# Placing the cluster rows of q and k by ScalarE in a routed-attention and expert-layer kernel

## The chip, the core and the metric

The kernel runs on one core of a Trainium2 chip. Its time is the device time in microseconds (us) of one execution, as a median of several. The core has five engines that this text names: TensorE (PE in the profile, with its weight loads apart as PEld), VectorE (DVE), ScalarE (ACT), GpSimd (POOL) and SyncE (SP), which here issues transfers. A letter q after an engine (ACTq, SPq) is its queue of instructions that don't compute, such as the issue of a transfer.

## The reference: what is computed

Two layers, one behind the other. The first is attention of 4 batches, 8 heads, 768 positions and 64 dimensions, in which a query sees only the keys of its own cluster. The cluster of a row of q or k is the nearest of 16 centroids of its head:

```python
q_assign = np.argmax(np.einsum('bhsd,hcd->bhsc', q_n, c_n), axis=-1)
k_assign = np.argmax(np.einsum('bhsd,hcd->bhsc', k_n, c_n), axis=-1)
mask = q_assign[:, :, :, None] == k_assign[:, :, None, :]
scores = scale * np.matmul(q, k.transpose(0, 1, 3, 2))
scores = np.where(mask, scores, -1000000000.0)
scores = scores - np.max(scores, axis=-1, keepdims=True)
attn = np.exp(scores)
attn = attn / (np.sum(attn, axis=-1, keepdims=True) + 1e-09)
return np.matmul(attn, v).astype(np.float32)
```

The second sends each of the 3072 rows that come out (512 wide) to one of 8 experts, two matrices with a relu between them, and scales the row by its gate. The change touches the first layer only.

## The kernel before

The attention works on 16 **groups**: a group is one batch and a pair of heads `a`. A group has 12 **units**, a unit being 128 keys against half of the queries (384) of both heads, and the units are worked in **turns** of six, so a group has two turns: turn 2g and turn 2g + 1. A turn is six scores, then the jobs of part 0, then six products with v, then the jobs of part 1:

```python
for n in range(-4, NTURN + 5):
    for x in range(n * NB, (n + 1) * NB):
        if 0 <= x < NU:
            score(x)
    for f, a in jobs.get((n, 0), ()):
        f(*a)
    for x in range(n * NB, (n + 1) * NB):
        if 0 <= x < NU:
            attend(x)
    for f, a in jobs.get((n, 1), ()):
        f(*a)
```

Each engine works through its own instructions in the order of this program.

The mask is a matmul. For each head, tile `ohT` holds in 32 partitions the one-hot cluster of every query, and for every key a large negative number everywhere but in its own cluster, where it is zero. A score is the product of q and k plus the product of these, then an exp:

```python
def score(u):
    ...
    ps = ps_s.tile([P, 2, 512], F32, name="sps")        # three buffers
    for a in range(2):
        r = slice(a * D, (a + 1) * D)
        nc.tensor.matmul(ps[:, a, 0:HS], lhsT=qk[g][r, 1, ks], rhs=qk[g][r, 0, qs], start=True, stop=False)   # L959
    for a in range(2):
        r = slice(a * D, (a + 1) * D)
        nc.tensor.matmul(ps[:, a, 0:HS], lhsT=ohT[g][r, 1, ks], rhs=ohT[g][r, 0, qs], start=False, stop=True) # L962
    A[u] = ap.tile([P, 2, HS], F32, name="A")
    nc.scalar.activation(A[u], ps[:, :, 0:HS], AF.Exp, scale=D**-0.5)                                         # L964
    ...  # T, the sum of A over the units of a half, by VectorE (L967, L971)
```

`attend` is the product with v (L979), `finish` ScalarE's copy of the product O out of its accumulator (L987).

The clusters come from `similar` (products with the centroids, brought out by VectorE as `sim`), `assign` and `assign2` (the largest of 16, as one-hot). They end in a tile `ohs` of 128 partitions: 32 for each of q and k and each half of the positions, with both heads side by side. To come into `ohT` the rows have to be put at other partitions, and for k the numbers have to be made of the one-hot: `big` holds a scale and a bias for each partition and head, which leave the other head's rows zero.

```python
def places(half, a):
    return slice(half * 32, half * 32 + 32), slice(a * D, a * D + 32), slice(half * HS, (half + 1) * HS)

def put_q(g):
    ohT[g] = ohTs[g % 2]
    for half in range(2):
        for a in range(2):
            i, r, cols = places(half, a)
            nc.sync.dma_start(out=ohT[g][r, 0, cols], in_=sims[g][i])                      # L917

def put_k(g):
    t, kv = sims.pop(g), asg.tile([P, 2, HS], BF16, name="kv")
    for a in range(2):
        nc.vector.tensor_scalar(                                                           # L923
            kv[D:P, a, :], t[D:P], scalar1=big[D:P, a, 0:1], scalar2=big[D:P, a, 1:2], op0=ALU.mult, op1=ALU.add
        )
    for half in range(2):
        for a in range(2):
            i, r, cols = places(half + 2, a)
            nc.sync.dma_start(out=ohT[g][r, 1, (half * HS) : (half + 1) * HS], in_=kv[i, a, :])  # L929
```

Group 0 has no transfers: `put` has ScalarE copy its four pieces of q (L939) and VectorE make its four of k.

The schedule of the jobs, as far as it matters here:

```python
for g in range(NG):
    n = g * TG                                   # TG = 2 turns a group
    ...
    elif g == 1:
        at(-2, 1, idle_of, 20)
        at(0, 0, turn_blocks, g)
        for f in (similar, assign, assign2, put_q, put_k):
            at(0, 1, f, g)
    else:
        at(n - 3, 0, turn_blocks, g)
        at(n - 2, 0, similar, g)
        at(n - 2, 0, assign, g)
        at(n - 2, 1, assign2, g)
        at(n - 2, 1, put_q, g)
        at(n - 2, 1, put_k, g)
    at(n, 1, finish, g, 0)
    at(n + 1, 1, finish, g, 1)
    if g < NG - 1:
        at(n + 2, 0, weigh, g)
        at(n + 2, 1, keep, g, 0, S)
        if g % HP == HP - 1:                     # the last pair of heads of a batch
            at(n + 3, 0, gate, g // HP)
            at(n + 3, 1, keep_pads, g // HP)
...
for e in range(2):
    for i in range(DB):                          # turns 5, 7, ... 19
        at(HP * TG * (e + 1) - 4 + 2 * i + 1, 0, early, e, i)
```

`early` has ScalarE issue two loads of expert weights (L1177). `gate` has VectorE take the largest logit and subtract (L1039, L1041), ScalarE exponentiate (L1044), and VectorE go on.

Of the kernel before, what the change touches and what calls it, by code (L numbers as in the profile page):

```python
# [9 lines left out]
BF16 = mybir.dt.bfloat16  # L10
I32 = mybir.dt.int32
AX = mybir.AxisListType.X
AF = mybir.ActivationFunctionType
ALU = mybir.AluOpType
# [171 lines left out]
def kernel(  # L186
# [11 lines left out]
    nc = tc.nc  # L198
    B, H, S, D = q.shape
    C = centroids.shape[1]  # L200
    P = 128
# [5 lines left out]
    HS = S // 2  # L207
# [25 lines left out]
    def fetch1(e, i):  # L233
        w1 = wpool.tile([P, DB, F], F32, name=f"w1_{i % 2}")
        nc.sync.dma_start(out=w1, in_=moe_w1[bass.ds(e, 1)].rearrange("e (a p) f -> p (e a) f", p=P))
        return w1

    def fetch2(e, i):
        w2 = wpool.tile([P, FB, Dm], F32, name=f"w2_{i % 2}")
        nc.sync.dma_start(out=w2, in_=moe_w2[bass.ds(e, 1)].rearrange("e (a p) d -> p (e a) d", p=P))  # L240
        return w2
# [459 lines left out]
    with ExitStack() as actx:  # L701
# [3 lines left out]
        asg = actx.enter_context(tc.tile_pool(name="asg", bufs=2))  # L705
# [78 lines left out]
        for i in range(2):  # L784
            t = ohp.tile([P, 2, S], BF16, name=f"ohT{i}")
            nc.gpsimd.memset(t, 0.0)
            ohTs.append(t)
        for a in range(2):
            r = slice(a * D, (a + 1) * D)
# [20 lines left out]
        for a in range(2):  # L810
# [6 lines left out]
            part_i, part_i, scalar1=4, scalar2=1, op0=ALU.arith_shift_right, op1=ALU.bitwise_and  # L817
        )
        big = consts.tile([P, 2, 2], F32)
# [14 lines left out]
        qk, sims, ohT = {}, {}, {}  # L834
# [72 lines left out]
        def places(half, a):  # L907

            return slice(half * 32, half * 32 + 32), slice(a * D, a * D + 32), slice(half * HS, (half + 1) * HS)

        def put_q(g):

            ohT[g] = ohTs[g % 2]
            for half in range(2):
                for a in range(2):
                    i, r, cols = places(half, a)
                    nc.sync.dma_start(out=ohT[g][r, 0, cols], in_=sims[g][i])  # L917

        def put_k(g):

            t, kv = sims.pop(g), asg.tile([P, 2, HS], BF16, name="kv")
            for a in range(2):
                nc.vector.tensor_scalar(  # L923
                    kv[D:P, a, :], t[D:P], scalar1=big[D:P, a, 0:1], scalar2=big[D:P, a, 1:2], op0=ALU.mult, op1=ALU.add
                )
            for half in range(2):
                for a in range(2):
                    i, r, cols = places(half + 2, a)
                    nc.sync.dma_start(out=ohT[g][r, 1, (half * HS) : (half + 1) * HS], in_=kv[i, a, :])  # L929

        def put(g):

# [127 lines left out]
        def at(n, part, f, *a):  # L1060
            jobs.setdefault((n, part), []).append((f, a))
# [8 lines left out]
        for g in range(NG):  # L1070
            n = g * TG
            if g == 0:
                at(-4, 0, turn, g, 0)
                at(-4, 0, load_next)
                at(-4, 0, blocks)
                at(-4, 1, turn, g, 1)
                at(-3, 0, similar, g)
                at(-3, 0, assign, g)
                at(-3, 0, assign2, g)
                at(-3, 0, put, g)  # L1080
            elif g == 1:
                at(-2, 1, idle_of, 20)
                at(0, 0, turn_blocks, g)
                for f in (similar, assign, assign2, put_q, put_k):
                    at(0, 1, f, g)
            else:
                at(n - 3, 0, turn_blocks, g)
                at(n - 2, 0, similar, g)
                at(n - 2, 0, assign, g)
                at(n - 2, 1, assign2, g)  # L1090
                at(n - 2, 1, put_q, g)
                at(n - 2, 1, put_k, g)
            at(n, 1, finish, g, 0)
            at(n + 1, 1, finish, g, 1)
            if g < NG - 1:
                at(n + 2, 0, weigh, g)
                at(n + 2, 1, keep, g, 0, S)
                if g % HP == HP - 1:
                    at(n + 3, 0, gate, g // HP)
                    at(n + 3, 1, keep_pads, g // HP)  # L1100
# [41 lines left out]
        n = (NG - HP) * TG  # L1142
# [13 lines left out]
        n = NG * TG  # L1156
# [46 lines left out]
    with tc.tile_pool(name="sm", bufs=1) as sm:  # L1203
# [20 lines left out]
        for part in parts:  # L1224
            n, over = part["n"], part["over"]
# [8 lines left out]
        for t0 in range(0, NT, TQ):  # L1234
# [34 lines left out]
            op0=ALU.is_ge, op1=ALU.add,  # L1269
# [53 lines left out]
    g = groups[0]  # L1323
# [49 lines left out]
    with tc.If(more > 0):  # L1373
        nx = nc.values_load(xe[0:1, NX : NX + 1], min_val=0, max_val=NX)
        general = nc.values_load(xe[0:1, NX + 1 : NX + 2], min_val=0, max_val=1)
        with tc.If(nx > XU):
            with ExitStack() as ectx:
# [3 lines left out]
                with tc.For_i(XU, nx, 1) as i:  # L1381
# [4 lines left out]
                    g = dict(  # L1386
                        n=[P], rows=N, w=(fetch1(ex, 0), fetch2(ex, 0)), gi=lambda j: gi[:, 0:1], si=lambda j: gi[:, 1:2], apart=False
                    )
# [37 lines left out]
```

## Time and profile before

| | |
|---|---|
| time, median of 3 | 713.92 us (713.08 to 714.17) |
| profiled span | 717.3 us, mean granted TensorE clock 0.994 |
| attention, 16 to 346 us | PE busy 323.30, DVE 279.01, ACT 166.78 of 330 us |
| ohT transfers | 60 from ohs, 60 from kv, 24 KB each, median 5.2 and 3.0 us to landing |
| kv on VectorE (L923) | 30 operations, median 386 ns |

A line of a group in the profile has: line of the program, engine, operation, what is written from what, shapes (partitions x elements), count | busy us, mean ns of one | idle us of the engine just before them, and what ended it. A line of waits has: who waited <- for whom, total us, times, longest us. A line of a timeline has: start us, us, engine, line, operation, count, and in brackets the idle time before it and its releaser.

### The profile page before, as it was taken

Reading aid. Unit: us, or ns where it says so; the run is one execution under the profiler, and the core shown is the slowest. Engines: PE = TensorE matmul, PEld = TensorE weight load, DVE = VectorE, ACT = ScalarE, POOL = GpSimd, SP = SyncE. Lnnn points to the kernel's source line nnn. Section 1 sums busy time; section 2 is a strip of 40 time slices with the busy share of each in tenths; the row PEclk is TensorE's granted clock in tenths of the full one; section 3 lists DMA queues with packets and bytes.
Section 4 is the critical chain, followed back from the end, with each engine's and each line's share of the span. In section 5 each row is a group of like instructions: output and inputs, shape, how many; then the busy total and the mean of one; then the engine's idle time right before and its main releaser. Section 6 shows DMA issues by size and latency. Waiting matters only on the chain.

```text
span 717.3 us, 12233 instructions
## 1 busy us (share of the span) xinstructions
PE 695.1 (97%) x4723; PEld 453.0 (63%) x4723; DVE 478.3 (67%) x761; ACT 255.8 (36%) x403; POOL 170.8 (24%) x262
## 2 busy tenths in 40 slices
PE   8999989999999999999999999999999999999993
PEld 6445444444444444545656969878798787888761
DVE  5898878798898889997456466565755667554200
ACT  3555445445544556445212222312214131231200
POOL 4022112222221122245235312112121221110101
PEclk9999999999999999999999999999999999999997
DMA  7355686668877555313135547485575855568440
GB/s 144 67 97 98 134 142 132 115 127 150 154 146 147 100 100 79 57 28 77 27 118 183 159 174 287 154 285 207 203 271 186 298 207 203 220 230 296 153 134 20
DMA packets 144164, 109.58 MB, mean 153 GB/s; under 512 B 106337, under 2 KB 114273, under 8 KB 144098
## 3 DMA queue, kind: packets, MB, share of 16 engines
q1 hardware_dynamic: 131042, 80.32, 41.5%
q0 software_dynamic: 7488, 19.57, 11.1%
q10 hardware_dynamic: 5568, 8.83, 4.3%
q8 instruction: 39, 0.64, 0.4%
q14 instruction: 27, 0.22, 0.1%
HBM read 93.01 MB, written 13.25 MB: 148 GB/s over the span
## 4 chain that ended last, share of the span: by engine, by line
PE 69%; issue 11%; DVE 8%; DMA 4%; SPq 3%; POOL 2%; ACT 1%; ACTq 0%; POOLq 0%; DVEq 0%
PE sps L959 12%; PE O L979 11%; PE sps L496 10%; PE sps L328 9%; PE sps L518 9%; PE sps L384 8%; PE sps L962 3%; DVE T L971 3%; DMA ohT<-kv 2%; PE sps L364 2%; PE mps L1002 2%; PE sps L309 2%; DMA k_in<-in_k_dram 1%; PE sps L873 1%; POOL out_dram L348 1%
## 5 line engine op out<-in xcount | busy, mean ns | idle before, releaser
L959 PE MATMUL sps<-qk 64*128 64x384 f32 x768 | 160.6, 494 | 1.4 <-DVE sim L880 1.4
L964 ACT ACTIVATE A<-sps 128x768 f32<-128x768 f32 x192 | 149.9, 814 | 20.9 <-PE sps L962 16.9
L971 DVE TENSOR_TENSOR T<-T,A 128x768 f32<-128x768 f32 x128 | 122.6, 958 | 14.6 <-DVE T L971 1.0
L979 PE MATMUL O<-A,v_in 128*64 128x384 f32 x768 | 130.9, 490 | 0.0
L959 PEld LDWEIGHTS sps<-qk 64*128 64x128 f32 x768 | 67.4, 186 | 52.4 <-issue 42.6
L979 PEld LDWEIGHTS O<-A,v_in 128*64 128x64 f32 x768 | 52.3, 137 | 74.0 <-issue 73.9
L962 PE MATMUL sps<-ohT 64*128 64x384 bf16 x384 | 67.0, 323 | 5.0 <-DMA ohT<-kv 5.0
L348 POOL DMA_INDIRECT out_dram<-zo,s_idx x32 | 33.4, 1043 | 154.1 <-ACT zo L344 93.6
L282 POOL DMA_INDIRECT xg<-x_rows,g_idx x32 | 38.1, 1189 | 115.6 <-ACT gate L302 65.1
L384 PE MATMUL sps<-w,h_sb 128*128 128x512 f32 x144 | 63.1, 592 | 0.0
L987 ACT COPY xT<-O 128x384 f32<-128x384 f32 x32 | 15.3, 478 | 132.8 <-PE O L979 100.3
L328 PEld LDWEIGHTS sps<-xgT,w 128*128 128x128 f32 x512 | 58.3, 192 | 4.5 <-issue 2.5
L328 PE MATMUL sps<-xgT,w 128*128 128x128 f32 x512 | 58.7, 275 | 0.0
L1014 POOL COPY dens<-ls 128x12 f32<-128x12 f32 x16 | 3.1, 194 | 211.9 <-DVE ls L1010 211.9
L1032 POOL DMA_DIRECT2D x_rows<-xb x68 | 48.4, 719 | 10.8 <-DVE xb L1029 8.8
L967 DVE SCALAR_TENSOR_TENSOR T<-A 128x768 f32<-128x768 f32 x32 | 30.6, 957 | 25.3 <-ACT A L964 24.8
L384 PEld LDWEIGHTS sps<-w,h_sb 128*128 128x128 f32 x144 | 26.7, 190 | 30.6 <-issue 30.6
L962 PEld LDWEIGHTS <-ohT 64*128 64x128 bf16 x384 | 22.1, 94 | 32.8 <-DMA ohT<-kv 10.4
L496 PEld LDWEIGHTS sps<-xs,w1s 128*128 128x128 f32 x288 | 36.0, 190 | 4.2 <-DVE xs L407 4.2
L496 PE MATMUL sps<-xs,w1s 128*128 128x144 f32 x288 | 37.8, 288 | 0.0
L344 ACT ACTIVATE zo<-sps,gate 128x512 f32<-128x512 f32 x12 | 8.2, 687 | 72.1 <-PE sps L384 53.5
L518 PE MATMUL sps<-w2s,hs 128*128 128x256 f32 x144 | 33.6, 383 | 0.0
(254 smaller groups left out, 905.4 us busy)
## 6 DMA issues: line engine op xcount, KB each, us to landing
w<-in_moe_w_dram SPq DMA_DIRECT2D x28, 2048.0 KB, 9.0
w<-in_moe_w_dram ACTq DMA_DIRECT2D x16, 512.0 KB, 5.6
v_in<-in_v_dram SPq DMA_DIRECT2D x16, 384.0 KB, 3.9
q_in<-in_q_dram SPq DMA_DIRECT2D x60, 96.0 KB, 3.5
k_in<-in_k_dram SPq DMA_DIRECT2D x60, 96.0 KB, 3.8
x_rows<-xb POOLq DMA_DIRECT2D x60, 96.0 KB, 4.4
ohT<-ohs SPq DMA_DIRECT2D x60, 24.0 KB, 5.2
ohT<-kv SPq DMA_DIRECT2D x60, 24.0 KB, 3.0
```

Source lines behind the costliest of these rows:

```text
L282: nc.gpsimd.indirect_dma_start(out=g["xg"][0:m, j, :], out_offset=None, in_=x_d[0 : g["rows"], :], in_offset=bass.IndirectOffsetOnAxis(ap= ...
L328: nc.tensor.matmul(o, lhsT=g["w"][0][:, c, fb * P : (fb + 1) * P], rhs=g["xT"][:, c, :cols], start=(c == 0), stop=(c == DB - 1),)
L348: ins = nc.gpsimd.indirect_dma_start(out=out[:, :], out_offset=bass.IndirectOffsetOnAxis(ap=g["si"](j)[0:m], axis=0), in_=zo[0:m], in_offs ...
L384: nc.tensor.matmul(zp, lhsT=g["h"][:, fb, j * P : (j + 1) * P], rhs=g["w"][1][:, fb, :], start=(fb == 0), stop=(fb == FB - 1),)
L496: nc.tensor.matmul(o, lhsT=a[:, c, f * P : (f + 1) * P], rhs=b[:, c, :], start=(c == 0), stop=(c == KH - 1),)
L518: nc.tensor.matmul(ps[:, 0, 0:DH], lhsT=a[:, f, :], rhs=b[:, f, :], start=(f == 0), stop=(f == FH - 1),)
L959: nc.tensor.matmul(ps[:, a, 0:HS], lhsT=qk[g][r, 1, ks], rhs=qk[g][r, 0, qs], start=True, stop=False)
L962: nc.tensor.matmul(ps[:, a, 0:HS], lhsT=ohT[g][r, 1, ks], rhs=ohT[g][r, 0, qs], start=False, stop=True)
L964: nc.scalar.activation(A[u], ps[:, :, 0:HS], AF.Exp, scale=D**-0.5)
L971: nc.vector.tensor_tensor(T[g, half], T[g, half], A[u], op=ALU.add)
L979: nc.tensor.matmul(O[g, half][a * D : (a + 1) * D, 0:HS], lhsT=rows[g, "v"][:, a, j, :], rhs=a_[:, a, :], start=(j == 0), stop=(j == NQ - 1),)
L1032: nc.gpsimd.dma_start(out=x_d[b * S + c0 : b * S + c1, d0 : d0 + 32].rearrange("(n t) d -> t n d", t=32), in_=xb[quad * 32 : (quad + 1) * ...
```

## The change

The cluster rows of q and k are no longer moved by transfers. ScalarE places them: a copy for each of the four pieces of q, and for each of the four pieces of k an activation (identity) that applies scale and bias of `big` on the way, so that VectorE makes no `kv`. It does so a turn later than the transfers were issued, in the second turn of the group ahead, behind that turn's six exponentials, where the engines' order has TensorE at the products with v and ScalarE waiting for them. It is meant to take the landing time of small transfers out of the way of the mask's matmul, and two operations a group off VectorE.

```diff
-        def put_q(g):
-
+        def put_by_scalar(g):
+
+            t = sims.pop(g)
             ohT[g] = ohTs[g % 2]
             for half in range(2):
                 for a in range(2):
                     i, r, cols = places(half, a)
-                    nc.sync.dma_start(out=ohT[g][r, 0, cols], in_=sims[g][i])
-
-        def put_k(g):
-
-            t, kv = sims.pop(g), asg.tile([P, 2, HS], BF16, name="kv")
-            for a in range(2):
-                nc.vector.tensor_scalar(
-                    kv[D:P, a, :], t[D:P], scalar1=big[D:P, a, 0:1], scalar2=big[D:P, a, 1:2], op0=ALU.mult, op1=ALU.add
-                )
-            for half in range(2):
-                for a in range(2):
-                    i, r, cols = places(half + 2, a)
-                    nc.sync.dma_start(out=ohT[g][r, 1, (half * HS) : (half + 1) * HS], in_=kv[i, a, :])
+                    k = slice(D + half * 32, D + half * 32 + 32)
+                    nc.scalar.copy(ohT[g][r, 0, cols], t[i])
+                    nc.scalar.activation(
+                        ohT[g][r, 1, cols], t[k], AF.Identity, scale=big[k, a, 0:1], bias=big[k, a, 1:2]
+                    )
...
             elif g == 1:
                 at(-2, 1, idle_of, 20)
                 at(0, 0, turn_blocks, g)
-                for f in (similar, assign, assign2, put_q, put_k):
+                for f in (similar, assign, assign2):
                     at(0, 1, f, g)
+                at(1, 0, put_by_scalar, g)
             else:
                 at(n - 3, 0, turn_blocks, g)
                 at(n - 2, 0, similar, g)
                 at(n - 2, 0, assign, g)
                 at(n - 2, 1, assign2, g)
-                at(n - 2, 1, put_q, g)
-                at(n - 2, 1, put_k, g)
+                at(n - 1, 0, put_by_scalar, g)
```

## The prediction

> **What bounds the kernel now.** I read the page first (busy shares, then groups), then the waits, then TensorE's and ScalarE's timelines of the attention part, which runs from about 16 to 346 us. On the page:
>
> ```profile
> PE 695.1 (97%) x4723; PEld 453.0 (63%) x4723; DVE 478.3 (67%) x761; ACT 255.8 (36%) x403; POOL 170.8 (24%) x262
> ...
> L962 PE MATMUL sps<-ohT 64*128 64x384 bf16 x384 | 67.0, 323 | 5.0 <-DMA ohT<-kv 5.0
> ```
>
> TensorE is the bound, and the only gaps in it that this change can reach are those ahead of L962, the matmul that adds the cluster mask. The waits of the span, and then TensorE's alone:
>
> ```profile
> ACT xT L987 <- PE O L979: 100.3, 24, 5.0
> ...
> PEld L962 <- DMA ohT<-kv: 10.4, 11, 2.5
> ```
> ```profile
> PE sps L962 <- DMA ohT<-kv: 5.0, 3, 1.9
> ...
> PE sps L959 <- DVE sim L880: 1.4, 1, 1.4
> ```
>
> ScalarE idles 100 us before its 24 copies of O, up to 5.0 us each: that is the room the change wants to use. TensorE's timeline shows the worst stall, at the start of group 4:
>
> ```profile
> 95.37 0.92 PE L959 MATMUL sps<-qk 64*128 64x384 f32 x4
> 98.19 0.54 PE L962 MATMUL sps<-ohT 64*128 64x384 bf16 x2 [1.91 <-DMA ohT<-kv]
> ```
>
> A group is two turns of six units. From TensorE's timeline, an undisturbed second turn takes 9.06 us (191.23 to 200.29: scores 5.04, products with v 4.02); the first adds weigh and similar, 10.82 us; a group is 19.88. Groups 1 to 15 start at 35.36, 55.47, 75.47, 95.37, 117.61, 138.00, 160.01, 180.10, 200.29, 220.18, 240.49, 260.38, 280.27, 300.70 and 323.01, and the last ends at 345.38. What each has over 19.88, less extra matmuls (0.54 in groups 13 and 14; +1.38 of turns and -0.65 of similar in the last) and less the 1.44 behind DVE's sim, is what the transfers cost: 0.23, 0.12, 0.02, 2.36, 0.51, 2.13, 0.21, 0.31, 0.01, 0.43, 0.01, 0.01, 0.01, 0.4, 1.75. **Sum 8.5 us**, 1.2% of the time: the ceiling of the direct gain.
>
> ScalarE around the start of group 9:
>
> ```profile
> 191.34 0.48 ACT L987 COPY xT<-O 128x384 f32<-128x384 f32 x1 [4.98 <-PE O L979]
> 192.37 4.82 ACT L964 ACTIVATE A<-sps 128x768 f32<-128x768 f32 x6 [0.55 <-PE sps L962]
> 200.24 0.24 ACT L1044 ACTIVATE ex<-ex 128x48 f32<-128x48 f32 x1 [3.04 <-DVE ex L1041]
> 200.32 0.84 ACTq L1177 DMA_DIRECT2D w<-in_moe_w_dram  x2
> 201.20 0.48 ACT L987 COPY xT<-O 128x384 f32<-128x384 f32 x1 [0.72 <-DMA ohT<-kv]
> 201.57 4.74 ACT L964 ACTIVATE A<-sps 128x768 f32<-128x768 f32 x6
> ```
>
> The exponentials of the second turn end 5.96 us after its start (197.19); the next are due 10.3 to 10.5 after it. The window is so some 4 us, with one copy (0.37 to the next start) in it. In this turn the gate's exp sits inside the window and waits for VectorE until 200.24, the window's end.
>
> **What the Trainium skill says.** "ScalarE: Activation LUTs", section "What ACT_TABLE_LOAD costs": each per-partition pointer for scale or bias adds about 93 ns to an ACTIVATE, and back-to-back ones overlap by about 93 ns. The groups of ScalarE by form agree on the first: 687 ns with a gate pointer, 594 without, the same shape. Section "Table sets: the hidden batching unit": identity and copy are in every set, so no table load; the trace has only its two loads at the start (1283 ns each), though it copies and exponentiates throughout. "DMA: Bandwidth & Descriptors", "Anatomy of one DMA — SWDGE (gpsimd) path": a semaphore wait happens on the issuing sequencer before dispatch. The trace agrees: the weight loads issued by ScalarE (L1177) start only once a kv transfer has landed (98.00 for the stall above), and hold the copy behind them.
>
> **The change, part by part.**
>
> *Removed:* 15 x 8 transfers, so the 8.5 us above; and two DVE operations per group, 15 x 0.80 = 12 us of VectorE. VectorE is not the bound: only its one late sim (1.44) is on the path, and kv work of 0.88 in the turn before plus the slack from below removes it. **Gain 8.5 + 1.4 = 9.9 us.**
>
> *Added:* eight ScalarE operations of 32x384 in one piece. From the groups by form, and from ScalarE's timeline for the same copies in group 0:
>
> ```profile
> L338 ACT ACTIVATE h_sb<-sps 128x512 f32<-128x512 f32 x16 | 8.7, 594 | 44.5 <-PE sps L328 44.5
> ...
> L344 ACT ACTIVATE zo<-sps,gate 128x512 f32<-128x512 f32 x12 | 8.2, 687 | 72.1 <-PE sps L384 53.5 <-issue 12.4 <-PEq L1373 6.2
> L344 ACT ACTIVATE zo<-zc,gate 32x512 f32<-32x512 f32 x8 | 5.8, 722 | 17.4 <-DVE zc L374 17.4
> ...
> L939 ACT COPY ohT<-ohs 32x384 bf16<-32x384 bf16 x4 | 2.0, 510 | 6.3 <-DVE ohs L905 6.2
> ...
> L338 ACT ACTIVATE hs<-sps 128x288 f32<-128x288 f32 x8 | 2.8, 408 | 12.0 <-PE sps L328 12.0
> ```
> ```profile
> 14.82 2.11 ACT L939 COPY ohT<-ohs 32x384 bf16<-32x384 bf16 x4 [6.23 <-DVE ohs L905]
> ```
>
> Four copies in 2.11 us: (2.11 - 0.51) / 3 = 0.533 from start to start, no overlap. The k operation: 722 (SBUF, one pointer, 512 long), less 128 x 0.83 (from 594 and 408 at 512 and 288), plus 93 for the second pointer = 709 ns, and the same 24 ns of gap: 0.733. Eight: 4 x 0.533 + 4 x 0.733 = **5.06 us**, more than the window.
>
> *What follows on the path.* In an ordinary group the eight end 5.96 + 5.06 = 11.02 after the second turn's start, the copy of O moves the first exp to 11.42, which is 2.36 into the next turn. TensorE has three score buffers: the fourth score starts 0.90 after the first exp starts (181.95 to 182.85 in group 8) and is due 2.52 into the turn (193.75 - 191.23), so an exp up to 1.62 in is free. Loss 2.36 - 1.62 = 0.74. The exps then follow closer (0.72) than scores (0.81), so it does not grow.
> - Groups 1, 2, 11, 12, 14: 5 x 0.74 = 3.7.
> - Groups 3, 4, 6, 7, 8, 10 also issue two weight loads after the eight. Transfers take eight completion counters in turn, so each waits for the one eight before it: today an ohT transfer, after the change a load long landed. So they no longer wait; they start 0.08 after the operation ahead of them starts, so of 0.84 only some 0.2 shows: 6 x 0.94 = 5.6.
> - Groups 5, 9, 13: the gate's exp is ahead of the eight in program order (it is appended for an earlier group, in the same part of the same turn). Its VectorE input ends at 117.87, 200.20, 279.84; without kv the chain of T additions starts earlier, but the first cannot start before the second exp's end (111.39, 194.07, 274.05), which saves 0.8, 0.57, 0.22. The exp so ends about 8.7 to 8.8 after the turn's start, the eight 13.8, the first exp at 14.2 to 14.5: losses 3.75, 3.65, 3.5 = 10.9. TensorE's first mask matmul, due at 9.8, waits there too, till about 11.2, inside the same loss.
> - Group 15: TensorE's own extras leave 0.2.
>
> **Sum: 3.7 + 5.6 + 10.9 + 0.2 = 20.4 lost, 9.9 gained: +10.5 us, 724.4.**
>
> **Rivals.**
> 1. *The operations overlap* by 0.1 each, as 128-row ones do (exps at 0.72 of 0.81). Then the eight take 4 x 0.41 + 4 x 0.61 = 4.08, ordinary groups lose nothing, the gates 0.98 less each, 8.0 in all; 9.9 gained: 712. Against it: all three pairs of exactly these copies show a gap of 24 ns.
> 2. *Only one pointer costs*, 0.64 a k operation: eight in 4.69, losses 5 x 0.37, 6 x 0.57 and 9.8: 15.1 lost, 719.
> 3. *As intended*: the gate's exp does not hold the eight (its input early, or another order): those three then lose 0.74 to 0.94 as others do, 12.1 in all, 716; with overlap as well, 704. Against: the 3.04 us wait at 200.24 is in the trace, and ScalarE runs in order.
> 4. *VectorE the bound*: its 12 us would count in full, 702. Against: it idles in each first turn waiting for A (22.6 us in all), so what it saves it waits.
>
> **Range and chances.** I give the sum above some two thirds, the cheaper rivals the rest: **722 us**, range 712 to 728. Over 2% slower needs 728.2, a dearer operation than any seen (each 0.1 us on the pitch adds 0.8 in 14 groups, 11 us): 0.09. Over 2% faster needs 699.6, more than all waits named: 0.02. Within: 0.89.
>
> **What would show it.** Right: no wait of L962 on a transfer; k operations near 0.7 us; the first exp of an ordinary group 2.3 to 2.4 us into its first turn, and TensorE held there by A; in groups 5, 9, 13 the eight start after the gate's exp, and L962 waits for ScalarE. Wrong: eight operations in 4 us; a gate's exp behind the eight; TensorE's groups at 19.9 throughout.

## The result, and the profile after

The changed kernel takes **727.01 us** (median of 4, 726.92 to 727.11) against 714.04 us (713.08 to 715.05) before: ratio 1.0181, 95% interval 1.0164 to 1.0199. It is slower by 13.0 us. The profiled spans, 717.3 us before and 725.4 after, differ by 8.1 only; the experiment "again" below settles why.

The page after: engines first, then the groups of the scores, of the mask's matmul, of ScalarE's copy of O and of the k operations. The columns are those of before; L952, L955, L957 and L980 are what L959, L962, L964 and L987 were.

```profile
PE 696.4 (96%) x4723; PEld 449.8 (62%) x4723; DVE 465.6 (64%) x731; ACT 324.6 (45%) x523; POOL 170.0 (23%) x262
...
L952 PE MATMUL sps<-qk 64*128 64x384 f32 x768 | 160.8, 496 | 10.3 <-ACT A L957 10.3
...
L955 PE MATMUL sps<-ohT 64*128 64x384 bf16 x384 | 64.7, 323 | 2.7 <-ACT ohT L920 2.7
...
L980 ACT COPY xT<-O 128x384 f32<-128x384 f32 x32 | 15.3, 478 | 80.6 <-PE O L972 80.2
...
L920 ACT ACTIVATE ohT<-ohs,big 32x384 bf16<-32x384 bf16 x60 | 42.0, 700 | 0.8
```

ScalarE is busy for 68.8 us more, VectorE for 12.7 less, TensorE as long as before. TensorE's waits show the exchange: none behind a transfer any more, and two behind ScalarE.

```profile
PE sps L952 <- ACT A L957: 10.3, 14, 1.7
PE sps L955 <- ACT ohT L920: 2.7, 3, 0.9
```

ScalarE's timeline over the start of group 12, which has neither a gate nor weight loads in its way. The second turn of group 11 starts on TensorE at 258.15, group 12 at 267.21.

```profile
259.26 4.85 ACT L957 ACTIVATE A<-sps 128x768 f32<-128x768 f32 x6 [0.52 <-PE sps L955]
264.14 0.51 ACT L919 COPY ohT<-ohs 32x384 bf16<-32x384 bf16 x1
264.67 0.70 ACT L920 ACTIVATE ohT<-ohs,big 32x384 bf16<-32x384 bf16 x1
265.39 0.51 ACT L919 COPY ohT<-ohs 32x384 bf16<-32x384 bf16 x1
...
268.39 0.70 ACT L920 ACTIVATE ohT<-ohs,big 32x384 bf16<-32x384 bf16 x1
269.12 0.48 ACT L980 COPY xT<-O 128x384 f32<-128x384 f32 x1
269.49 4.41 ACT L957 ACTIVATE A<-sps 128x768 f32<-128x768 f32 x6
```

The eight stand from 264.14 to 269.09, 4.95 us, while TensorE's products with v take 4.02. The first exp of the new group starts 2.28 us into it. TensorE's timeline shows what that does: the fourth score, the first that needs a buffer back, starts 0.87 us after that exp.

```profile
267.21 0.92 PE L952 MATMUL sps<-qk 64*128 64x384 f32 x4
...
270.36 0.92 PE L952 MATMUL sps<-qk 64*128 64x384 f32 x4 [0.46 <-ACT A L957]
```

It starts 3.15 us into the turn and not 2.52, and its first pair of matmuls, behind the pause, takes another 0.10 us (587 ns each for 482). Ordinary groups take 20.61 or 20.62 us (group 2 20.69) where an undisturbed one takes 19.89.

In groups 5, 9 and 13 the gate's exp is ahead. ScalarE's timeline at the start of group 9, then TensorE's (the second turn of group 8 starts at 193.79):

```profile
194.91 4.86 ACT L957 ACTIVATE A<-sps 128x768 f32<-128x768 f32 x6 [0.52 <-PE sps L955]
202.16 0.24 ACT L1037 ACTIVATE ex<-ex 128x48 f32<-128x48 f32 x1 [2.39 <-DVE ex L1034]
202.31 0.49 ACT L919 COPY ohT<-ohs 32x384 bf16<-32x384 bf16 x1
...
204.07 0.84 ACTq L1170 DMA_DIRECT2D w<-in_moe_w_dram  x2
...
206.54 0.70 ACT L920 ACTIVATE ohT<-ohs,big 32x384 bf16<-32x384 bf16 x1
207.27 0.48 ACT L980 COPY xT<-O 128x384 f32<-128x384 f32 x1
207.64 4.47 ACT L957 ACTIVATE A<-sps 128x768 f32<-128x768 f32 x6
```
```profile
202.86 0.92 PE L952 MATMUL sps<-qk 64*128 64x384 f32 x4
...
204.82 0.33 PE L955 MATMUL sps<-ohT 64*128 64x384 bf16 x1 [0.89 <-ACT ohT L920]
...
208.51 0.92 PE L952 MATMUL sps<-qk 64*128 64x384 f32 x4 [1.75 <-ACT A L957]
```

ScalarE idles 2.39 us in the very window the change wants to fill, and then does the eight when the next group has begun. The mask's matmul waits for the rows, and the fourth score for its buffer: the group takes 23.12 us.

### The profile page after: what moved, and what is told of

Read it like the earlier page. It is cut to its first block, busy times and chain, and to the rows that moved or that the text cites. A ratio compares the mean times of both kernels' runs of the same rounds, so it can differ in the third digit from the quotient of the medians.

```text
span 725.4 us, 12157 instructions
## 1 busy us (share of the span) xinstructions
PE 696.4 (96%) x4723; PEld 449.8 (62%) x4723; DVE 465.6 (64%) x731; ACT 324.6 (45%) x523; POOL 170.0 (23%) x262
## 4 chain that ended last, share of the span: by engine, by line
PE 73%; issue 10%; ACT 7%; DVE 5%; POOL 2%; DMA 1%; ACTq 0%; SPq 0%; POOLq 0%; DVEq 0%
PE sps L952 13%; PE O L972 13%; PE sps L496 10%; PE sps L328 9%; PE sps L518 9%; PE sps L384 8%; ACT A L957 3%; PE sps L955 3%; DVE T L964 3%; PE mps L995 2%; PE sps L364 2%; PE sps L309 2%; PE sps L873 1%; ACT ohT L920 1%; ACT ohT L919 1%
## 5 line engine op out<-in xcount | busy, mean ns | idle before, releaser
L952 PE MATMUL sps<-qk 64*128 64x384 f32 x768 | 160.8, 496 | 10.3 <-ACT A L957 10.3
L957 ACT ACTIVATE A<-sps 128x768 f32<-128x768 f32 x192 | 147.1, 818 | 12.4 <-PE sps L955 11.2
L964 DVE TENSOR_TENSOR T<-T,A 128x768 f32<-128x768 f32 x128 | 122.6, 958 | 14.3 <-ACT ohT L920 0.5
L952 PEld LDWEIGHTS sps<-qk 64*128 64x128 f32 x768 | 66.0, 186 | 67.6 <-issue 37.8
L955 PE MATMUL sps<-ohT 64*128 64x384 bf16 x384 | 64.7, 323 | 2.7 <-ACT ohT L920 2.7
L980 ACT COPY xT<-O 128x384 f32<-128x384 f32 x32 | 15.3, 478 | 80.6 <-PE O L972 80.2
L920 ACT ACTIVATE ohT<-ohs,big 32x384 bf16<-32x384 bf16 x60 | 42.0, 700 | 0.8
L955 PEld LDWEIGHTS <-ohT 64*128 64x128 bf16 x384 | 20.1, 94 | 28.6 <-ACT ohT L920 4.7
```

Of the source, the lines that this page charges most:

```text
L920: nc.scalar.activation(ohT[g][r, 1, cols], t[k], AF.Identity, scale=big[k, a, 0:1], bias=big[k, a, 1:2])
L964: nc.vector.tensor_tensor(T[g, half], T[g, half], A[u], op=ALU.add)
```

## The experiments

Theory A: TensorE waits for ScalarE's chain in the second turn (the eight, the copy of O, the exp), and where the gate's exp stands ahead of the eight the chain starts late. Rivals: B, the added ScalarE work costs as such, wherever it stands; C against D, on why medians and profiles differ; E, the loss is capped; F, VectorE is the bound. Ratios are to the kernel before in the same batch of runs; that kernel's own median was between 713.9 and 716.2 us. The changed kernel was timed in an earlier batch, so what a run gains on it is given by the profiled spans too.

**The kernel before, once more.** No edit.

> The kernel before, unchanged, profiled once more. The change gained +8.1 us by the two profiled spans (717.3 to 725.4) but +13.0 by the medians. Theory C: the profiled execution of before that the prediction was read from had some 5 us more of stalls behind the ohT transfers than most executions have, because landings vary from execution to execution. Then a new profile has a span of 711 to 714 us and its groups have 3 to 5 us in all over 19.88 us each, instead of 8.5. Rival D: a profiled execution of before is slower everywhere or always stalls as much. Then the span is 717 again with 8 to 9 us of stalls, or the extra lies outside the attention.

Measured: 715.64 us beside 716.16 (ratio 0.9996, 0.9988 to 1.0004), a span of 713.5 us. TensorE's waits:

```profile
PE sps L962 <- DMA ohT<-kv: 2.9, 3, 1.5
PE sps L959 <- DVE sim L880: 1.6, 1, 1.6
```

Worked out as in the prediction, from group starts, the transfers cost 4.8 us here, where the profile it read had 8.5: group 4 takes 21.48 us and not 22.24, group 6 20.49 and not 22.01, and five groups that had lost 0.2 to 0.5 lose nothing. The attention as a whole is 3.5 us shorter and the span 3.8. The transfers land sooner, at most 6.4 (from ohs) and 4.2 us (from kv) after their issue instead of 7.8 and 5.7. C holds: the stalls behind the transfers differ from execution to execution, and the profile of before was a bad one. The times say the same: in this batch 43 executions of before took 714.56 to 718.07 us, and 22 of six_two below, which has no such transfers, 715.61 to 715.94. The stalls themselves are measured in two executions only.

**The gate behind the eight.**

```diff
-                    at(n + 3, 0, gate, g // HP)      # in the loop over g: ahead of put_by_scalar of group g + 2
+        for g in range(HP - 1, NG - 1, HP):          # behind the loop
+            at(g * TG + 3, 0, gate, g // HP)
```

> The changed kernel, with the gate's jobs behind the eight placing operations in their turn instead of ahead of them. Theory A (ScalarE's chain in the second turn is what TensorE waits for, and the gate's exp, which waits for VectorE, holds the eight up in groups 5, 9 and 13): those groups lose 0.74 us like the others instead of 3.24, perhaps 0.9 for the exp itself; 3 x 2.4 = 7.2 us less than the changed kernel, 719.8 us. Rival B (the loss is the added ScalarE work as such, or loads and VectorE work brought forward, and not its place): 725 to 727.

Measured: 719.63 us (719.55 to 719.80), ratio 1.0041 (1.0029 to 1.0053); 7.4 less than the changed kernel, and by the spans 7.5 (717.9 for 725.4). The wait for rows is gone and the longest wait for an exp is 0.6 us:

```profile
PE sps L952 <- ACT A L957: 6.4, 14, 0.6
```

The order of two jobs of one engine in one turn was worth 7.4 of the 18 us that the eight cost (summed from the group starts below).

**Two of the eight a turn later.**

```diff
-                    nc.scalar.copy(ohT[g][r, 0, cols], t[i])
+                    if half == 0:
+                        nc.scalar.copy(ohT[g][r, 0, cols], t[i])
...
+        def put_rest(g):                             # q of the second half
+            t = sims.pop(g)
+            for a in range(2):
+                i, r, cols = places(1, a)
+                nc.scalar.copy(ohT[g][r, 0, cols], t[i])
...
+                at(n, 0, put_rest, g)
```

> The changed kernel, with the two copies of the second half of q, which the group needs only in its own second turn, placed one turn later; six operations stay in the turn ahead. The gate stays ahead. Theory A: the chain is 2 x 0.533 = 1.07 us shorter, the first exp of a group starts 1.3 us into its first turn, under the 1.62 that are free: eleven groups lose nothing instead of 0.73 and three lose 2.2 instead of 3.24: 11 us less than the changed kernel, 716 us. Rival B: the same operations, the same time, 726 to 727.

Measured: 715.76 us (715.61 to 715.94), ratio 0.9992 (0.9986 to 0.9999); 11.3 less than the changed kernel, by the spans 11.4. Ten of the eleven groups take 19.89 us, as undisturbed; group 14 takes 20.69, 0.26 over its undisturbed 20.43, and the three behind a gate 22.08 instead of 23.12 (group 13, which has 0.54 of its own extra matmuls, 22.62). The same 120 operations as in the change are done, so B falls: it is the place and not the work. The waits that are left behind ScalarE are those three groups':

```profile
PE sps L963 <- ACT ohT L921: 2.7, 3, 0.9
PE sps L960 <- ACT A L965: 2.1, 3, 0.7
```

**Both edits.**

> Both edits. Theory A: no group waits for ScalarE and no transfers are left to wait for, so the attention is at TensorE's own pace: 727.0 - 11 x 0.73 - 3 x 3.24 - 0.2 = 709 us, against 714.0 before (faster by 0.7%). Rival B: 725 to 727. If it is 714 or more, then the transfers cost before nothing in an ordinary execution.

Measured: 711.11 us, ratio 0.9922 (0.9909 to 0.9935): faster than before, but 2 us over what was expected. 1.4 of them are groups 5 and 9, which still lose 0.71 each, and 0.75 are group 14, whose second turn waits again for a late sim (0.5 us). For groups 5 and 9 VectorE's timeline shows why: the edit had moved the gate's subtraction (L1042) as well, behind the two transposes of q and k.

```profile
113.47 0.97 DVE L859 STREAM_TRANSPOSE qk<-q_in 128x768 f32<-128x768 f32 x1
114.37 0.94 DVE L859 STREAM_TRANSPOSE qk<-k_in 128x768 f32<-128x768 f32 x1
115.23 0.16 DVE L1040 TENSOR_REDUCE lmax<-lg 128x6 f32<-128x48 f32 x1
115.42 0.21 DVE L1042 TENSOR_TENSOR ex<-lg,lmax 128x48 f32<-128x48 f32 x1
```

(The expectation of the next run calls these "groups 4 and 8 in TensorE's count"; they are the groups 5 and 9 of this text, counted from the starts of group 1 on.)

**The gate split.** Subtraction where it was, exp and the rest behind the placing.

```diff
-                    at(n + 3, 0, gate, g // HP)
+                    at(n + 3, 0, gate_v, g // HP)    # VectorE: largest logit, subtraction
...
+        for g in range(HP - 1, NG - 1, HP):
+            at(g * TG + 3, 0, gate_s, g // HP)       # ScalarE: exp; VectorE: sum, reciprocal
```

> As six_two_gate_last, but VectorE's part of the gate (largest logit, subtraction) is back ahead of its transposes of q and k, and only the exp and what follows are behind the placing operations. In six_two_gate_last groups 4 and 8 in TensorE's count still lost 0.71 us each, because the exp waited for VectorE, whose subtraction had moved behind two transposes of 0.95 us. Theory A: that input is now ready before the six operations end, so both 0.71 vanish: 711.1 - 1.4 = 709.7 us. Rival: the exp's 0.24 us and the two weight loads issued behind it cost as before: 711.

Measured: 709.71 us (709.60 to 709.78), ratio 0.9939 (0.9926 to 0.9952). Groups 1 to 12 take 19.89 us each. ScalarE at the start of group 5 (second turn from 105.69, group 5 from 114.75):

```profile
106.82 4.83 ACT L965 ACTIVATE A<-sps 128x768 f32<-128x768 f32 x6 [0.55 <-PE sps L963]
111.67 0.51 ACT L920 COPY ohT<-ohs 32x384 bf16<-32x384 bf16 x1
...
115.61 0.24 ACT L1050 ACTIVATE ex<-ex 128x48 f32<-128x48 f32 x1
115.76 0.46 ACT L988 COPY xT<-O 128x384 f32<-128x384 f32 x1
116.12 1.51 ACT L965 ACTIVATE A<-sps 128x768 f32<-128x768 f32 x2
```

Six placing operations, the exp and the copy follow without a gap, and the first exp of the group starts 1.37 us into it, inside the 1.62 that are free. Of the 18.0 us that the eight cost, 17.3 are gone (727.01 to 709.71), so the place of the eight and of the gate's exp accounts for nearly all of it, and the rival's 711 falls. This version beats both kernels.

**Ten operations instead of eight.** Two copies more, of values already placed.

```diff
+            for a in range(2):
+                i, r, cols = places(1, a)
+                nc.scalar.copy(ohT[g][r, 0, cols], t[i])
```

> The changed kernel with two more copies of the same kind behind the eight (the second half of q written once more, the same values). Theory A: the stay of ScalarE in the second turn is paid one for one once it is over the room: 2 x 0.533 = 1.07 us more in each of 14 groups and some 0.9 in the last, 16 us more than the changed kernel, 743 us. Rival E (TensorE's loss comes in steps or is capped, because later exponentials catch up): under 735.

Measured: 746.35 us (745.04 to 746.69), a span of 743.2. The groups of the changed kernel grow from 20.61 to 21.71, 1.10 for 1.07 of work: one for one, so E falls. The total is 3 us over what was expected. Half of that is in the profile, in group 5, which takes 25.84 us and not 24.22 as group 9 does. Stretches of that group, each with its length, the busy time of PE, PEld, DVE, ACT and POOL with their counts, then the granted clock, the share of DMA and its GB/s:

```profile
126.00:128.00 2.00, 0.00 (x0) 0.00 (x0) 0.00 (x0) 1.93 (x5) 0.00 (x0) 1.00 1.16 273
...
130.00:131.00 1.00, 1.00 (x8) 0.55 (x6) 0.90 (x2) 0.87 (x2) 0.00 (x0) 0.59 1.09 336
131.00:132.00 1.00, 1.00 (x6) 0.38 (x4) 0.90 (x2) 0.81 (x1) 0.00 (x0) 0.50 1.16 292
132.00:133.00 1.00, 1.00 (x12) 0.26 (x12) 0.90 (x2) 0.28 (x1) 0.00 (x0) 0.50 1.46 177
133.00:134.00 1.00, 1.00 (x24) 0.67 (x20) 0.90 (x2) 0.54 (x1) 0.00 (x0) 0.70 0.45 59
134.00:135.00 1.00, 1.00 (x18) 0.33 (x12) 1.00 (x2) 0.00 (x0) 0.00 (x0) 1.00 0.44 64
```

TensorE pauses for 2.84 us, waiting for A, and a little later works for some 3.4 us at half its clock. The other two executions took 1.3 and 1.65 us more than the profiled one and show a lower mean granted clock, 0.990 for 0.992, which fits one more such stretch in each; that it was one isn't shown.

**k by VectorE.** The gate split; ScalarE copies q's four pieces, VectorE places k's four.

```diff
-                    nc.scalar.activation(
-                        ohT[g][r, 1, cols], t[k], AF.Identity, scale=big[k, a, 0:1], bias=big[k, a, 1:2]
-                    )
+                    nc.vector.tensor_scalar(          # in turn n - 2, part 1
+                        ohT[g][r, 1, cols], t[k], scalar1=big[k, a, 0:1], scalar2=big[k, a, 1:2], op0=ALU.mult, op1=ALU.add
+                    )
```

> The four copies of q by ScalarE in the second turn as in the change, but k's four values placed by VectorE straight behind its transpose (four operations of 0.40 us from start to start, 1.6 us a group), the gate split as in six_two_gate_split. Theory A: ScalarE's chain is 2.1 us, no loss there; VectorE has room in each first turn, except around groups 13 to 15, where its sim is late by 1.6 us more: 711 to 712 us. Rival F (VectorE is the real bound of the attention, as its busy share of nine tenths suggests): 15 x 1.6 us = 24 us over six_two_gate_split, 734.

Measured: 715.68 us, ratio 1.0024 (1.0015 to 1.0032). F's 734 does not come, but the expected 711 to 712 was too low by 4. Against six_two_gate_split the attention is 5.3 us longer: 2.7 in group 14, whose second turn waits for a sim,

```profile
PE sps L959 <- DVE sim L880: 2.6, 1, 2.6
PE sps L959 <- ACT A L964: 1.0, 1, 1.0
```

1.3 in group 5, where VectorE's four placing operations (1.74 us) made the gate's subtraction late again (it ends 10.7 us into the turn, and in six_two_gate_split 8.3), 0.2 in group 9, and 1.1 in the last. The medians differ by 6.0; the executions of this kernel with the lowest mean clock, 0.989, took 716.74 and 717.26 us, those at 0.995 at most 715.17. VectorE has room on average, but not in every turn.

**kv put back, transfers left out.** six_two_gate_split with the two kv operations of before on VectorE, their result unused.

```diff
+            if g > 0:
+                kv = asg.tile([P, 2, HS], BF16, name="kv")
+                for a in range(2):
+                    nc.vector.tensor_scalar(
+                        kv[D:P, a, :], sims[g][D:P], scalar1=big[D:P, a, 0:1], scalar2=big[D:P, a, 1:2], op0=ALU.mult, op1=ALU.add
+                    )
```

> six_two_gate_split with VectorE's two kv operations of before put back in their old place, their result unused, so that of the change only the transfers are left out. The prediction held that VectorE's saving counts only where its sim is late, ahead of group 15 (1.4 us). Theory A: 709.7 + 1.0 to 1.4 = 711 us; the rest of the gain over before is the transfers'. Rival F (VectorE bounds the attention): 15 x 0.80 = 12 us more, 722.

> six_two_gate_split once more, on the same chip as split_kv, for the comparison: 709.7 us on either chip, as it hangs on no transfer's landing in the attention; a second profile with every group from 1 to 12 at 19.89 us again.

Measured on one chip: 710.64 us (710.46 to 710.75) with kv, 709.52 (709.43 to 709.68) without. VectorE's 12 us are worth 1.1 us. What VectorE saves it waits, first without kv, then with:

```profile
DVE T L968 <- ACT A L965: 30.2, 26, 2.1
```
```profile
DVE T L974 <- ACT A L971: 18.2, 12, 2.1
```

TensorE's waits with kv have sim at 1.1 us,

```profile
PE sps L966 <- DVE sim L880: 1.1, 1, 1.1
```

and without kv at 0.3:

```profile
PE sps L960 <- DVE sim L880: 0.3, 1, 0.3
```

In both, groups 1 to 12 take 19.89 us. The kernel before, beside them, took 716.06 us (715.03 to 718.80): 5.4 of the 6.5 us between it and six_two_gate_split remain with kv in place, so they go with the transfers. Without them the time also hardly varies: 709.43 to 709.78 over the two batches, where before ran from 713.08 to 718.80 over all, and took 719.12 in the execution whose profile the prediction read.

## Why the prediction was right or wrong

**The range held (712 to 728), the middle (722) was 5 us too fast.** The steps one by one:

*Eight operations of 32x384 take longer than the window.* Right: 4.95 us against 5.06 worked out. The k operation took 700 ns for 709, and the gaps between the eight are 11 to 25 ns, where 24 had been taken from group 0. So the rivals of overlap (4.08 us) and of one pointer (4.69) fall. Here the trace also bears on the Trainium skill, "ScalarE: Activation LUTs", section "What ACT_TABLE_LOAD costs": that each pointer operand costs about 93 ns agrees with 700 ns; that back-to-back ACTIVATEs overlap by about 93 ns, measured there on tiles of 128 partitions, is not seen in these of 32: in six_two, where one k operation directly follows another, it starts 13 to 27 ns after the end of the one ahead.

*An exp up to 1.62 us into a turn is free, and beyond that TensorE pays one for one.* Right: 0.73 us in ordinary groups (0.74 predicted), nothing with six in ten of the eleven, 1.10 more with ten operations.

*The weight loads add 0.2 to each of six groups.* Wrong, they add nothing: 0.73 there too. The step had the issue start one operation ahead. In the trace it starts with the fourth of the eight (204.07 above) in all eight groups with loads, so all 0.84 us of it lie beside the other four. They no longer wait for ohT transfers, as predicted: the counter that the load at 204.07 takes had its last transfer landed at 193.04, and the one of the load at 98.00 in before at 97.98. (That one was a transfer of q, from ohs, and not of kv as the prediction reads it; the mechanism is the same.)

*The gate's exp holds the eight up in groups 5, 9 and 13.* Right in kind and place, and gate_last shows it. The size was 3.2 us each and not 3.5 to 3.75: the exp ended 8.6 us into the turn and not 8.7 to 8.8, and the eight took 0.1 less. Rival 3, which had another order or an early input, falls.

*Sum of the losses:* predicted 20.4. Measured from the group starts: 8.0 in eleven groups, 9.7 in three, 0.3 in the last: 18.0.

*Gain of 9.9 us.* This is the step that failed for the time. Its mechanism was right: no transfer is waited for, and in the changed kernel no late sim either (at the faster pace of six_two_gate_split 0.3 us of it come back). But 8.5 of the 9.9 were read off one execution in which transfers landed late more often than usual. By the profiled spans the change loses 18.0 and gains 9.9, 8.1, which is the 8.1 they differ by. By the medians it loses 13.0, so an ordinary execution had only some 5 us to give: in the batches above, before is 4.2 and 6.5 us over six_two_gate_split. The profiled run of before had a sign of it: it took 719.12 us where the runs without it took 713.08 to 714.17, and the prediction took the stalls from the one and the starting time from the others.

*VectorE's 12 us are not on the path.* Right, and shown by split_kv: 1.1 us, about the 1.4 predicted; with kv VectorE waits 18.2 us for A, without it 30.2.

The two errors of the sum, 2.4 too much lost and some 5 too much gained, partly cancelled; that the worked 724.4 came within 2.6 us of the measured time is in part luck. The step from there to 722, for the sake of cheaper operations, went the wrong way, since the trace had already shown these operations at their price.

## What to carry to other kernels

Work moved into the idle time of an engine is free only up to the slack of what that engine does next: measure the window up to the moment its next result is needed, add the moved operations one by one with the duration of the same shape, and look for anything already in the window that waits. When the sum is over, split the work by when each piece is needed: here a quarter of it could wait one turn, and that quarter and the order of one other job made the difference between 1.8% slower and 0.6 to 0.9% faster.

When a gain is read as waits behind transfers, read it from more than one execution. If the profiled run's own time is above those of the other runs, as here (719.12 us against at most 714.17), its waits may be above theirs as well.

## What was not expected of the hardware

ScalarE's queue took up the issue of two loads (0.84 us) with four operations ahead of it still to run, when none of them had to wait: in group 9 at 204.07, with the fourth of the eight, while the last of them started at 206.54. In six_two too four were still to run, in "ten" two. In the kernel before, behind an exp that had to wait, it started 0.08 us after that exp.

In "ten", a long pause cost more than itself: behind 2.84 us without a matmul the granted clock fell to 0.50 for some 3.4 us (from about 130.2), and the group took 1.6 us more than group 9, which has the same pause and kept its clock (1.00 from 208 to 234). The Trainium skill, "TensorE: Matmul & The Clock Gate", section "Part 1: The HAM clock gate (the "warmup" mystery)", has TensorE's clock halved behind an idle window of about 3.4 us, with windows that run free of the kernel's start. The half rate, and that one of equal pauses is hit and another is not, agree with it; the pause itself was shorter than the page's window. One case in one profile doesn't settle when it strikes.
